# A fused attention and two-MLP kernel: seven products per tile pair in another order

## The chip, the cores and the metric

One Trainium2 chip, one core of it. The metric is the device time of one execution in microseconds (us). Before the change it is 658.96 us, the median of three runs (658.83 to 658.99).

## What is computed

All data are float32. The output of one layer is the input of the next:

```python
scores = q @ k.T / 8 - log(448);  attn = 1 / (1 + exp(-scores));  x = attn @ v    # 4 x 12 heads, 448 x 64
x = max(x @ w1, x @ w2, x @ w3) @ moe_w_out                                      # 1792 x 768, inner 768
h = x @ moe2_w_in                                                                 # 1792 x 1024
solu = h * softmax(h);  ln = (solu - mean) / sqrt(var + 1e-6) * g_ln
out = ln @ moe2_w_out                                                             # 1792 x 768
```

The change lies in the second MLP, in the product that gives `h`.

## The kernel before, in words

**Stages.** Attention runs first. In its course the kernel multiplies `moe_w_out` by `moe2_w_in`, so that the first MLP's maximum feeds `h` directly through a merged weight. Then come the three products of the first MLP with their maximum (`product`, line 634, and `sums`, line 652). The second layer has two stages: stage L gives `h` (with softmax and normalization behind it), stage O gives the output.

**Products.** Every large product is a seven-product scheme of the Strassen-Winograd kind on 2 x 2 blocks. A unit is a pair of token tiles (256 rows), and there are seven units, numbered 0 to 6 (called L0 to L6 in stage L, O0 to O6 in stage O). The seven products P1 to P7 of a unit each multiply one of seven token operands (A11, A12, S2, S1, S3, A22, S4) by one of seven weight operands; `PROD` (line 38) has the pairs. Every operand is split into a high and a low part, and a block takes three matmuls (high-high, high-low, low-high). A product is 9 matmuls of 512 columns in stage L and 12 of 384 columns in stage O (`product_c`, line 940).

**Running sums.** X collects P1, then P6, then P7, then P4. After P1, P6 and P7 ScalarE copies the sum as it stands (lines 1122, 1142, 1153), and after P4 it is read once more. The next product into X has to wait until the copy has read it. V collects P5, then P3, and is read by VectorE after P5 and after P3. Z holds P2. PSUM has three buffers for X, two for V, two for Z.

**Order of the work around the change.** The loop from line 1169 walks over groups: L0 to L6, then O0 with O1 together, then O2 to O6. A group of stage L runs on TensorE, with the last two products of the unit before in its first half: P1 of this unit (`begin`), P4 (`fourth`) and P3 (`third`) of the unit before (both called in `close`, line 1109), P2 (`second`), P6 (`sixth`), P5 (`fifth`), P7 (`seventh`). The orders of TensorE, ScalarE and VectorE are those of the program's text, and each of them takes its instructions in that order.

**Background work.** Two queues of small steps are woven between the matmuls. `bg` holds `prep` (line 788), which makes the seven operands of the next unit: ScalarE casts the high part (line 51), VectorE subtracts for the low part (line 56) and forms sums (line 59). `lazy` holds `solu_ln` (line 980): two Exp, two multiplies, two Square, some tiny steps, two Identity, two transposes, and the write of the result to DRAM, from which stage O's operands are loaded (`load_u`, line 1027). `third` of a unit of stage L puts that unit's `solu_ln` into `lazy` as its last act. After each matmul `pace` (line 934) adds 0.227 (L) or 0.174 (O) to a credit, and while it is positive one step is called and its cost taken off (0.56 or 0.69 for a step of `prep`, 1.32 for a multiply, 1.25 for a transpose, 0.78 for reading a finished sum by VectorE):

```python
while credit["t"] > 0:
    if not step(bg) and not step(lazy):
        credit["t"] = 0.0
```

So `lazy` gets a step only where `bg` has none that can be done, and credit is dropped where both are empty. `prep` of the next unit is put into `bg` after five products of a group (line 1206). If a product finds its operand not made yet, `product_c` calls steps of `bg` until it is (line 943). The operands lie in a ring of ten buffers (`place`, line 757). One of stage O takes two, so each takes over the buffers of the operand five places before it, and can be made only when the product that uses that one has been issued. `in_turn` (line 842) alternates between the `prep` of O0 and of O1.

Of the kernel before, what the change touches and what calls it, by code (L numbers as in the profile page):

```python
# [44 lines left out]
def sigmoid_attention_max_moe_solu_ln(tc, q, k, v, w123, wo, wi, w2, g, out):  # L45
# [12 lines left out]
    def tt(dst, a, b, op):  # L58
        dve.tensor_tensor(out=dst, in0=a, in1=b, op=op)
# [8 lines left out]
    def shut(*cms):  # L68
        for cm in cms:
            cm.__exit__(None, None, None)  # L70
# [563 lines left out]
    def product(ps, u, name, start, stop):  # L634
        gi, bp = u
        a, bn = PROD[name]
        while (gi, a) not in wops or any((bp, bn, c) in fts for c in range(3)):
            run_bg()
        wt = wops[(gi, a)]
        for c in range(3):  # L640
            xh, xl = xops[bp][(bn, c)]
            wh, wl = (wt[:, i, c * P : (c + 1) * P] for i in range(2))
            for i, (l, r) in enumerate(((wh, xh), (wh, xl), (wl, xh))):
                pe.matmul(ps, lhsT=l, rhs=r, start=(start and c == 0 and i == 0), stop=(stop and c == 2 and i == 2), skip_group_check=True)  # L644
                tick["n"] += 1
                if c == 2 and i == 2:
                    used[(gi, a)] = used.get((gi, a), 0) + 1
                while tick["done"] < tick["n"] * tick["rate"]:
                    run_bg()
                    tick["done"] += 1  # L650
# [73 lines left out]
    def weight_slots(name, tags, side="left"):  # L724
        cm, p = open_pool(name, 1, side=side)
        slot_pools.append(cm)
        return {tag: p for tag in tags}
# [9 lines left out]
    def load_wf(nm, tag):  # L737
        t = wfs[("L", nm)] = wslot[tag].tile([P, 3, 2, 512], F32R, tag=f"s{tag}", name=f"wf{nm}")
        pool.dma_start(out=t.bitcast(F32).rearrange("p c a b -> p c (a b)"), in_=w_d[nm][:, :, : 2 * 512])
# [181 lines left out]
    def step(queue):  # L921

        while queue:
            cost = next(queue[0], "end")
            if cost == "end":
                queue.popleft()
                continue
            if cost is None:
                return False
            credit["t"] -= cost  # L930
            return True
        return False
# [7 lines left out]
    def product_c(ps, kind, p, name, start, stop):  # L940
        a, bn = PROD[name]
        key = (kind, p, a)
        while key not in cops:
            assert step(bg), key
        hl = cops.pop(key)
        wt = wfs[(kind, bn)]
        chunks, dt = (3, 0.227) if kind == "L" else (4, 0.174)
        for c in range(chunks):
            for i, (l, m) in enumerate(((0, 0), (0, 1), (1, 0))):
                pe.matmul(  # L950
                    ps,
                    lhsT=hl[l][:, c * P : (c + 1) * P],
                    rhs=wt[:, c, m],
                    start=(start and c == 0 and i == 0),
                    stop=(stop and c == chunks - 1 and i == 2),
                    skip_group_check=True,
                )
                if c == chunks - 1 and i == 2:
                    spent.add(key)
                pace(dt)  # L960

    def charge(cost):
        credit["t"] -= cost
# [9 lines left out]
    def add_min(dst, ps, other, low, first):  # L973

        dve.tensor_tensor_reduce(
            out=dst, in0=ps, in1=other, scale=-1.0, scalar=first, op0=ALU.add, op1=ALU.min, accum_out=low
        )
        charge(0.78)
# [48 lines left out]
    def load_u(p):  # L1027
        for t in tiles[2 * p : 2 * p + 2]:
            while t not in turned:
                step(bg)  # L1030
                assert step(lazy), t
            ut = (hfirst if p == 0 else tp).tile([P, 4, 256], F32, tag="hu", name=f"ut{t}", bufs=2 if p == 0 else 11)
            sp.dma_start(out=ut, in_=u_d[t].rearrange("b f i e -> (b f) i e"))
            uts[t] = ut.rearrange("p i (k t) -> p k i t", k=K2)
# [23 lines left out]
    def put_out(p, i, j, t):  # L1058
        r = tiles[2 * p + i]
        sp.dma_start(out=out[r * P : (r + 1) * P, j * HU : (j + 1) * HU], in_=t)  # L1060
# [12 lines left out]
    def release(kind, p, name):  # L1073

        if (kind, p) == ("L", NP2 - 1):
            n = LOADS.index(PROD[name][1])
            if n + 1 < len(LOADS):
                load_w2(LOADS[n + 1], n)

    def fourth(o):  # L1080
        kind, p = o["kind"], o["p"]
        cx = o["at"][3]
        product_c(o["X"], kind, p, "P4", False, True)
        release(kind, p, "P4")
        if kind == "L":
            first, low = (x[:, 1:] for x in sts[p][:2])
            dve.tensor_scalar(
                out=cx, in0=o["X"], scalar1=-1.0, scalar2=first, op0=ALU.mult, op1=ALU.min, accum_out=low
            )
            charge(0.78)  # L1090
        else:
            act.copy(cx, o["X"])
            put_out(p, 1, 0, cx)

    def third(o):
        kind, p = o["kind"], o["p"]
        u2 = o["at"][1]
        product_c(o["V"], kind, p, "P3", False, True)
        release(kind, p, "P3")
        if kind == "L":  # L1100
            first, low = (x[:, :1] for x in sts[p][:2])
            add_min(u2, o["V"], u2, low, first)
            lazy.append(solu_ln(p))
        else:
            tt(u2, o["V"], u2, ALU.add)
            charge(0.56)
            put_out(p, 0, 1, u2)

    def close(units):

        if len(units) == 1:
            fourth(units[0])
        for o in units:
            third(o)

    def begin(kind, p):
        w = 512 if kind == "L" else HU
        at = targets(kind, p)
        X = ps_x.tile([P, 512], F32, tag="x", name=f"X{kind}{p}")[:, :w]
        product_c(X, kind, p, "P1", True, False)  # L1120
        release(kind, p, "P1")
        act.copy(at[0], X)
        return dict(kind=kind, p=p, X=X, at=at, w=w)
# [15 lines left out]
    def sixth(o):  # L1139
        product_c(o["X"], o["kind"], o["p"], "P6", False, False)  # L1140
        release(o["kind"], o["p"], "P6")
        act.copy(o["at"][1], o["X"])
# [25 lines left out]
    prev = None  # L1168
    for n, (kind, g) in enumerate(groups):
        p, last = g[-1], n == len(groups) - 1  # L1170
        if prev and len(prev) > 1:
            for o in prev:
                fourth(o)
        now_open = [begin(kind, g[0])]
        if n == 0:
            product(old["X"], old["u"], "P4", False, True)
            sums(old["u"], 1, 0, old["X"], None)
            product(old["V"], old["u"], "P3", False, True)
            sums(old["u"], 0, 1, old["V"], old["u2"])
            for cm in (xat_cm, xau_cm, xa_cm, st_cm, raw_cm):  # L1180
                shut(cm)
            wslot.update(weight_slots("sc", (5, 6, 7), side="right"))
            for tag in (5, 6):
                load_wf(LOADS[tag], tag)
            t_cm, tp = open_pool("tp", 2, side="right")
            act.preload_act_table_set("natural_log_exp_and_others")
        else:
            close(prev)
        now_open += [begin(kind, p) for p in g[1:]]
        if n == 2:  # L1190
            load_w2(LOADS[0], 7)
        if (kind, p) == ("L", NP2 - 1):
            load_u(1)
        if not last:
            for o in now_open:
                second(o)
        if (kind, p) == ("O", 1):
            load_u(2)
        for o in now_open:
            sixth(o)  # L1200
        if kind == "L":
            if p + 2 < NP2:
                next_h(p + 2)
            if p == NP2 - 2:
                load_u(0)
            bg.append(prep_l(p + 1) if p + 1 < NP2 else in_turn(prep_o(0), prep_o(1), 1))
        elif not last:
            bg.append(prep_o(p + 1))
            if 1 < p < NP2 - 2:
                load_u(p + 2)  # L1210
        for o in now_open:
            fifth(o)
        for o in now_open:
            seventh(o)
        if (kind, p) == ("O", 1):
            load_u(3)
        if last:
            for o in now_open:
                second(o)
        prev = now_open  # L1220
# [61 lines left out]
```

## Time and profile before

| what | value |
|---|---|
| device time, median of 3 runs | 658.96 us |
| the profiled execution's own time | 658.38 us |
| its span, first to last instruction | 656.6 us |
| TensorE matmul busy | 637.8 us, 97% |
| VectorE busy | 490.7 us, 75% |
| ScalarE busy | 373.4 us, 57% |
| stage L, first product to the first of stage O | 427 to 544 us |
| stage O, to the end | 544 to 656.6 us |
| mean granted TensorE clock | 0.992 |

Busy shares are means over the whole span; in a timeline a row's number in front is its start in us from the span's start, then its duration, and in brackets the time the engine was idle before it and what released it.

### The profile page before, as it was taken

Reading aid. Unit: us, or ns where it says so; the run is one execution under the profiler, and the core shown is the slowest. Engines: PE = TensorE matmul, PEld = TensorE weight load, DVE = VectorE, ACT = ScalarE, POOL = GpSimd, SP = SyncE. Lnnn points to the kernel's source line nnn. Section 1 sums busy time; section 2 is a strip of 40 time slices with the busy share of each in tenths; the row PEclk is TensorE's granted clock in tenths of the full one; section 3 lists DMA queues with packets and bytes.
Section 4 is the critical chain, followed back from the end, with each engine's and each line's share of the span. In section 5 each row is a group of like instructions: output and inputs, shape, how many; then the busy total and the mean of one; then the engine's idle time right before and its main releaser. Section 6 shows DMA issues by size and latency. Waiting matters only on the chain.

```text
span 656.6 us, 9719 instructions
## 1 busy us (share of the span) xinstructions
PE 637.8 (97%) x3283; PEld 519.3 (79%) x3283; DVE 490.7 (75%) x1070; ACT 373.4 (57%) x712; POOL 72.6 (11%) x147
## 2 busy tenths in 40 slices
PE   9999999999999999999999999977999999999897
PEld 6555588754557999999999999955877889999897
DVE  4799987599547788886888678544688879687672
ACT  5888523578866545455455454222666674766551
POOL 2111121000100101101101100112000035300000
PEclk9999999999999999999999999997999999999999
DMA  8688668853710346765468543899336269956151
GB/s 292 216 256 260 220 199 303 314 211 109 259 33 0 105 125 188 215 166 163 131 176 233 168 121 90 248 374 407 130 108 182 58 205 385 311 180 185 59 168 70
DMA packets 85921, 125.17 MB, mean 191 GB/s; under 512 B 39024, under 2 KB 65648, under 8 KB 85872
## 3 DMA queue, kind: packets, MB, share of 16 engines
q1 hardware_dynamic: 74288, 70.84, 34.2%
q0 software_dynamic: 11440, 53.48, 25.2%
q8 instruction: 26, 0.43, 0.3%
q10 hardware_dynamic: 144, 0.23, 0.1%
q14 instruction: 23, 0.19, 0.1%
HBM read 84.15 MB, written 40.37 MB: 190 GB/s over the span
## 4 chain that ended last, share of the span: by engine, by line
PE 65%; DVE 16%; ACT 6%; DMA 6%; issue 5%; SPq 1%; POOL 0%; DVEq 0%; ACTq 0%; POOLq 0%
PE x L644 19%; PE v L644 9%; PE XO L950 7%; PE av L272 6%; PE z L644 5%; PE XL L950 5%; PE sc L251 4%; PE VO L950 4%; PE VL L950 2%; PE ZO L950 2%; DMA wfT<-w_dT 2%; ACT e L998 2%; PE sc L247 1%; DMA wfB<-w_dB 1%; ACT h L1014 1%
## 5 line engine op out<-in xcount | busy, mean ns | idle before, releaser
L272 PE MATMUL av<-sf,vr 128*64 128x448 f32 x384 | 77.5, 545 | 0.0
L259 ACT ACTIVATE sf<-sc,bias_s 128x896 f32<-128x896 f32 x72 | 67.9, 1013 | 2.4
L141 POOL DMA_DIRECT2D raw<-in_w x52 | 28.0, 539 | 277.3 <-DVE S L56 138.4
L272 PEld LDWEIGHTS av<-sf,vr 128*64 128x64 f32 x384 | 25.4, 136 | 40.9 <-issue 34.4
L251 PE MATMUL sc<-qt,kt 64*128 64x448 f32 x432 | 51.1, 375 | 1.5 <-ACT sf L256 1.5
L473 PE MATMUL pw<-wi_t,r_wo 128*128 128x512 f32 x216 | 49.6, 390 | 0.0
L251 PEld LDWEIGHTS sc<-qt,kt 64*128 64x128 f32 x432 | 39.0, 184 | 11.7 <-issue 4.3
L473 PEld LDWEIGHTS pw<-wi_t,r_wo 128*128 128x128 f32 x216 | 40.4, 188 | 9.4 <-issue 1.0
L689 ACT COPY u<-x 128x448 f32<-128x448 f32 x36 | 19.1, 530 | 44.3 <-PE x L644 44.3
L950 PE MATMUL XL<-wfT,c_L_S 128*128 128x512 f32 x126 | 33.1, 409 | 4.1 <-DMA wfT<-w_dT 3.1
L644 PE MATMUL x<-T3h,S 128*128 128x448 f32 x108 | 33.7, 366 | 0.0
L644 PE MATMUL x<-B11h,A 128*128 128x448 f32 x108 | 33.7, 366 | 0.0
L644 PE MATMUL x<-T4h,A 128*128 128x448 f32 x108 | 33.6, 365 | 0.0
L644 PE MATMUL x<-T2h,S 128*128 128x448 f32 x108 | 33.6, 365 | 0.0
L644 PE MATMUL v<-B22h,S 128*128 128x448 f32 x108 | 33.6, 365 | 0.0
L644 PE MATMUL z<-B21h,A 128*128 128x448 f32 x108 | 33.6, 365 | 0.0
L644 PE MATMUL v<-T1h,S 128*128 128x448 f32 x108 | 33.6, 365 | 0.0
L950 PEld LDWEIGHTS XL<-wfT,c_L_S 128*128 128x128 f32 x126 | 24.3, 196 | 11.3 <-issue 4.2
L413 ACT ACTIVATE raw<-raw,g_sb 128x192 f32<-128x192 f32 x32 | 13.3, 466 | 31.3 <-DVE raw L157 31.3
L950 PE MATMUL XO<-w2tT,c_O_S 128*128 128x384 f32 x168 | 31.1, 336 | 0.0
L157 DVE SCALAR_TENSOR_TENSOR raw<-raw 128x384 int32<-128x384 int32 x52 | 29.0, 557 | 1.1
L950 PEld LDWEIGHTS XO<-w2tT,c_O_S 128*128 128x128 f32 x168 | 29.3, 188 | 0.0
(185 smaller groups left out, 1547.1 us busy)
## 6 DMA issues: line engine op xcount, KB each, us to landing
raw<-in_w POOLq DMA_DIRECT2D x52, 384.0 KB, 4.1
w_d<-w2s SPq DMA_DIRECT2D x48, 192.0 KB, 2.4
u_d<-h SPq DMA_DIRECT2D x56, 128.0 KB, 2.9
ut<-u_d SPq DMA_DIRECT2D x14, 512.0 KB, 5.3
kr<-in_k SPq DMA_DIRECT2D x24, 256.0 KB, 3.5
vr<-in_v SPq DMA_DIRECT2D x24, 256.0 KB, 3.9
raw<-in_wi POOLq DMA_DIRECT2D x16, 384.0 KB, 4.9
w_dT<-wsT SPq DMA_DIRECT2D x12, 512.0 KB, 3.7
```

Source lines behind the costliest of these rows:

```text
L141: pool.dma_start(out=t, in_=source(key).rearrange("p (n t) -> p n t", t=2))
L157: dve.scalar_tensor_tensor(out=yi, in0=raws[key][:, cols, 0], scalar=29, in1=yi, op0=ALU.logical_shift_right, op1=ALU.bitwise_or)
L247: pe.matmul(sc[:, 0, :S], lhsT=kt[:, x, c * P :], rhs=qt[:, y], start=start, stop=stop)
L251: pe.matmul(sc[:, j, :S], lhsT=kt[rows, x, c * P : (c + 1) * P], rhs=qt[rows, y], start=start, stop=stop)
L259: act.activation(sf, sc[:, :, :S], AF.Sigmoid, bias=bias_s, scale=1.0 / math.sqrt(D))
L272: pe.matmul(pa[j * D : (j + 1) * D, :S], lhsT=vr[:, j, c], rhs=sf if c == 3 else sf[:, j], start=(n == 0), stop=(n == 3),)
L413: act.activation(half, half, AF.Copy, scale=g_sb[:, kc + 4 * i : kc + 4 * i + 1])
L473: pe.matmul(ps, lhsT=wt[:, a, cols], rhs=wi_t[:, b, c0 : c0 + 512], start=(i == 0), stop=(i == 3 * KC - 1))
L644: pe.matmul(ps, lhsT=l, rhs=r, start=(start and c == 0 and i == 0), stop=(stop and c == 2 and i == 2), skip_group_check=True)
L689: act.copy(e, ps)
L950: pe.matmul(ps, lhsT=hl[l][:, c * P : (c + 1) * P], rhs=wt[:, c, m], start=(start and c == 0 and i == 0), stop=(stop and c == chunks - 1 a ...
L998: act.activation(e[i], h[i], AF.Square, bias=su[:, c], scale=-float(F2), accum_out=vs[:, c])
```

## The change

In stage L, from the second unit on, P4 and P3 of the unit before no longer follow P1 directly. P4 goes behind P2, P3 behind P6. The order P1, P4', P3', P2, P6, P5, P7 (a prime marks the unit before) becomes P1, P2, P4', P6, P3', P5, P7. The group in which O0 begins still closes L6 as before, and stage O's order is not touched. `prep` of the next unit still goes into `bg` after five products; the step that puts `solu_ln` of the unit before into `lazy` now stands directly ahead of that, where it had stood two products ahead. No instruction is added or removed.

```diff
             t_cm, tp = open_pool("tp", 2, side="right")
             act.preload_act_table_set("natural_log_exp_and_others")
-        else:
+        elif kind == "O":
             close(prev)
         now_open += [begin(kind, p) for p in g[1:]]
...
         if (kind, p) == ("O", 1):
             load_u(2)
+        if n > 0 and kind == "L":
+            fourth(prev[0])
         for o in now_open:
             sixth(o)
+        if n > 0 and kind == "L":
+            third(prev[0])
         if kind == "L":
```

## Rows read from the trace of the kernel before

**Rows 1.** The page, part 1: busy time, share of the span, instructions.

```profile
PE   637.8 (97%) x3283; PEld 519.3 (79%) x3283; DVE 490.7 (75%) x1070; ACT 373.4 (57%) x712; POOL 72.6 (11%) x147
```

**Rows 2.** Waits of PE from 440 us on: total, times, longest.

```profile
PE VL L950 <- DMA wfB<-w_dB: 1.9, 1, 1.9
PE XO L950 <- ACT u L1153: 1.7, 1, 1.7
PE XL L950 <- ACT h L1153: 0.4, 1, 0.4
```

**Rows 3.** Timeline of PE, 435 to 463 us: P2, P6, P5, P7 of L0, and on.

```profile
435.01 2.35 PE L950 MATMUL ZL<-wfB,c_L_A 128*128 128x512 f32 x9 [1.92 <-DMA wfB<-w_dB]
...
440.12 3.09 PE L950 MATMUL XL<-wfT,c_L_S 128*128 128x512 f32 x9 [2.77 <-DMA wfT<-w_dT]
445.57 4.21 PE L950 MATMUL VL<-wfT,c_L_S 128*128 128x512 f32 x9 [2.35 <-DMA wfT<-w_dT]
450.07 3.04 PE L950 MATMUL XL<-wfT,c_L_S 128*128 128x512 f32 x9 [0.29 <-DMA wfT<-w_dT]
452.95 2.22 PE L950 MATMUL XL<-wfB,c_L_A 128*128 128x512 f32 x9
455.02 2.29 PE L950 MATMUL XL<-wfT,c_L_A 128*128 128x512 f32 x9
459.21 2.32 PE L950 MATMUL VL<-wfB,c_L_S 128*128 128x512 f32 x9 [1.89 <-DMA wfB<-w_dB]
461.36 2.22 PE L950 MATMUL ZL<-wfB,c_L_A 128*128 128x512 f32 x9
```

**Rows 4.** Timeline of PE: P5 and P7 of L2, P1 of L3.

```profile
479.93 2.23 PE L950 MATMUL VL<-wfT,c_L_S 128*128 128x512 f32 x9
483.12 2.33 PE L950 MATMUL XL<-wfT,c_L_S 128*128 128x512 f32 x9 [0.96 <-ACT h L1142]
485.29 2.23 PE L950 MATMUL XL<-wfB,c_L_A 128*128 128x512 f32 x9
```

**Rows 5.** Timeline of ACT just before that: the second Exp and the copy behind it.

```profile
481.37 1.14 ACT L988 ACTIVATE e<-h,st 128x1024 f32<-128x1024 f32 x1
482.50 0.56 ACT L1142 COPY h<-XL 128x512 f32<-128x512 f32 x1
```

**Rows 6.** Timeline of ACT: the first Exp of L0, and L6's first square and its Identity.

```profile
462.36 1.15 ACT L988 ACTIVATE e<-h,st 128x1024 f32<-128x1024 f32 x1 [6.56 <-DVE st L975]
...
614.38 1.15 ACT L998 ACTIVATE e<-h,st 128x1024 f32<-128x1024 f32 x1
...
618.63 2.37 ACT L1014 ACTIVATE h<-h,st 128x1024 f32<-128x1024 f32 x2 [1.02 <-DVE st L1010]
```

**Rows 7.** Timeline, 572 to 574 us: O2's first two casts, and its P1.

```profile
572.16 1.14 ACT L51 CAST c_O_A<-ut 128x512 fp32r<-128x512 f32 x2
573.67 2.27 PE L950 MATMUL XO<-w2tB,c_O_A 128*128 128x384 f32 x12
```

**Rows 8.** Groups by line: busy us, mean ns of one, idle before and its releaser.

```profile
L1018 DVE STREAM_TRANSPOSE h<-h 128x1024 f32<-128x1024 f32 x14 | 17.3, 1240 | 7.3 <-ACT h L1014 7.3
L56 DVE TENSOR_TENSOR c_O_A<-ut,c_O_A 128x512 fp32r<-128x512 f32 x21 | 14.3, 686 | 5.8 <-ACT c_O_A L51 4.5 <-PE VO L950 1.0 <-PE ZO L950 0.2
L51 ACT CAST c_O_A<-ut 128x512 fp32r<-128x512 f32 x21 | 12.7, 618 | 0.9 <-PE VO L950 0.9
L59 DVE TENSOR_TENSOR u<-VO,u 128x384 f32<-128x384 f32 x14 | 7.7, 550 | 10.1 <-ACT u L1153 5.9 <-PE VO L950 4.0
```

**Rows 9.** Timeline of PE and ACT: two products of stage O, and the copy of the first.

```profile
611.21 2.24 PE L950 MATMUL XO<-w2tT,c_O_S 128*128 128x384 f32 x12
613.29 2.24 PE L950 MATMUL VO<-w2tT,c_O_S 128*128 128x384 f32 x12
613.49 0.48 ACT L1142 COPY u<-XO 128x384 f32<-128x384 f32 x1 [3.54 <-PE XO L950]
```

**Rows 10.** A window of 1 us: PE, PEld, DVE, ACT, POOL busy, then granted clock.

```profile
442.00:443.00 1.00, 1.00 (x3) 0.40 (x2) 0.00 (x0) 0.00 (x0) 0.00 (x0) 0.50 1.07 423
```

## The prediction

> **What bounds the kernel now.** I read the page's busy shares first [rows 1]: TensorE is busy for 97% of the span, so a reordering can at most return the gaps, and any new gap is paid in full. Then the waits of TensorE, which say what the gaps are [rows 2]. From 440 us on, the change can reach one wait of 1.9 us for a weight's transfer and the waits for a ScalarE copy of a running sum: 0.4 us and one of 1.0 us in stage L [rows 4], 1.7 us in stage O. Then the timeline at two of them. At 459.21 us P3 of L0 waits for its weight [rows 3]. At 483.12 us P7 of L2 waits for the copy behind P6 [rows 4], and the copy is late only because an Exp of `solu_ln` stands ahead of it in ScalarE's queue [rows 5]. So it is background work, not the copy's own 0.56 us, that holds TensorE, and where that work is issued decides what the change is worth.
>
> **What is taken away.** A product of stage L starts 2.07 us after the one before it (452.95 to 455.02) [rows 3].
> 1. P3 of L0 moves behind P1, P2 and P6 of L1 and P4 of L0. In the old order it could have started at 457.1 us; in the new one its turn comes two products later, at 461.2 us, after the weight's arrival at 459.2 us. From 455.02 to 461.36 us are 6.34 us for two products that need 4.14: 2.2 us gone [rows 3]. The weight's load is issued by POOL, whose order is not touched, and SP's loads of the next rows still go out after five products, so I cost both moves at nothing; their cover is a whole group of some 14 us.
> 2. P7 of L2: 485.29 less 479.93 is 5.36 us for two products, 1.2 us over [rows 4]. The wait for the copy behind P7, 0.4 us by the view, is some 0.7 us by the same count (start-up is 0.25 us there). Two more on copies, too short for the view, are at most 0.5 us each; I take 0.8 together. With one more product between, all are covered: 2.7 us.
>
> In sum 4.9 us are to be had; the lower bound is 2.2, if ScalarE falls further behind.
>
> **What is moved with it: the background account.** P3's last act puts the unit's `solu_ln` into the lazy queue. In the old order two products (18 x 0.227 = 4.1 of credit) followed before the next unit's `prep` went in ahead of it. In the new order `prep` follows at once. So in the group of L1 both queues run empty while P4, P6 and P3 go by, and the credit is dropped; the loss is never made up, since a group gives 63 x 0.227 = 14.3 and asks for four readings (3.1), a `prep` (6.3) and a `solu_ln` (6.7), 16.1 in all. I carried the account step by step through both orders with the program's own costs. For the old order it puts the first Exp of L0 into P2 of L1, which ends at 463.4 us, and the squares of L6 behind P6 of O4 as steps forced by the load of their tiles; the trace has them there [rows 6]. For the new order it gives, at the end of L6, the `solu_ln` of L3 not yet finished, where before that of L4 had begun: some 2.7 of cost later. What is late next are stage O's operands, at five places.
>
> The prices: a cast 0.62, a subtraction or sum 0.69, a transpose 1.24, a VectorE reading 0.55 us [rows 8]; a product of stage O takes 2.08 us, its copy 0.48, and the copy starts 0.2 us after the product's end (613.49 against 613.29) [rows 9]. A product's first two matmuls (0.35 us) need the high part alone.
> 1. P1 of O0: between P6 of L6 and the cast of A11 ScalarE now has a copy, the whole tail of L3's `solu_ln` from the first square to the second Identity, and the cast. The tail of L6 takes 6.6 us (614.38 to 621.00), of which VectorE's small steps are 1.0 [rows 6]. So 0.2 + 0.5 + 6.6 + 0.6 = 7.9 us, against P3, P5, P7 = 6.2 us on TensorE. With the low part (0.69 - 0.35) a wait of 2.1 us; 2.3 with start-up.
> 2. P1 of O2: its buffers are those of the operand five places before. In the old order that is A22 of O0, so the cast ran at 572.16 us, 1.5 us ahead of P1 [rows 7]. In the new order the two alternating preparations come out otherwise, and it is A22 of O1, free only at the end of P4 of O1, directly ahead of P1. ScalarE is then still at two Identity and a copy. From the end of P7 of O0 it has four copies (1.9), the tail without VectorE's part (5.6) [rows 6] and two casts (1.1) [rows 7]: 8.6 us, some 8.4 as neighbours overlap a little, against three products, 6.2 us. Behind the second Identity, transpose and subtraction on VectorE end 0.5 us after copy, cast and the first two matmuls (1.24 + 0.69 - 0.48 - 0.62 - 0.35): 2.7 us.
> 3. P2 of O2: A12 needs P3 of O1 issued, then reading 0.55, sum 0.69, subtraction 0.69, with 0.2 ahead and 0.35 off: 1.8; 2.0 with start-up.
> 4. P6 of O2: reading, two sums, cast, subtraction after P2's end: 0.2 + 0.55 + 1.4 + 0.6 + 0.35 = 3.1 us.
> 5. P1 of O3: copy, reading, subtraction: 0.2 + 0.48 + 0.55 + 0.69 - 0.35 = 1.6 us.
>
> With 0.6 us for three small ones: 12.3 us. The old 1.7 us wait stays: the squares of L6 are forced at the same place. Bounds: a quarter less (9.2), if chains overlap better than end to end, and a fifth more (14.8), if ScalarE's queue is longer than I count.
>
> **The clock.** Nowhere in stage O does the trace before show gaps so close, so I bound this from both sides. In L0 the granted clock went from 1.00 to 0.50 (2.4 to 1.2 GHz) after waits of 1.9 and 2.8 us with one product between [rows 3, 10], and was back at 452.95 us, where a product takes 2.22 us again. P6, P5 and P7 took 3.09, 4.21 and 3.04 us instead of 2.22 each: 3.7 us [rows 3]. The waits of 1.0 and 1.7 us [rows 2, 4], and the single one of 1.89 us at 459.21 us, where the product behind took 2.32 us [rows 3], cost no clock. Places 3 and 4 are 2.0 and 3.1 us with one product between, which is nearest to L0; but three products then run without a break, where L0 had two more waits in them. I take half, 1.7 us, between 0 and 3.7.
>
> The Trainium skill, TensorE: Matmul & The Clock Gate, A second HAM failure mode: psum-queue depth-cycling, has frequent short idles between groups of matmuls swing the clock between its levels; by it the sum would carry not one fall but several, up to the last rival below. The trace agrees only in part: the single waits just named left the clock alone.
>
> **The sum.** -4.9 + 12.3 + 1.7 = 9.1 us. The profiled execution's own 658.38 us becomes 667.5 (its span 665.7). It lies 0.6 us below the median, so 668.1 us, called 668.0.
>
> **The rivals.**
> - *The clock holds.* Operands are late as above and nothing else: 658.96 + 7.4 = 666.4 us. For it: 6.2 us of unbroken work before place 3. Against: L0.
> - *The clock falls and stays.* Rising only after the wait at place 5, it costs L0's full 3.7 us: 670.1 us. For it: the waits at 3, 4 and 5 come 8 us apart at most, as in L0.
> - *The other side: the operands stay hidden.* If operands of O2 are cast before their products as in the old order [rows 7], the gaps go and none comes: 658.96 - 4.9 = 654.1 us. It decides at P1 of O2: a cast of its A11 ahead of the end of P4 of O1 would show it. For it: VectorE is only 75% busy [rows 1]. Against: steps are placed by credit and ring, not by who is idle.
> - *It does nothing.* The copies stay late because Exp and squares move along with them, and only the 2.2 us at 459 us are gained and lost again at O0: 659 us. Against: the account's four places in O2 and O3.
> - *The clock swings all along*, low from place 2 to place 5: eight products of 2.08 us take twice that, 7.4 + 16.6, 683 us. For it: four waits in 24 us. Against: between places 2 and 3 lie three products without a break. It is the case that the Trainium skill's section above would give.
>
> **How the numbers follow.** Forecast 0.42, clock holds 0.30, clock falls and stays 0.13, clock swings 0.03, hidden 0.07, nothing 0.05 (0.02 same, 0.03 slower). Low end: no clock term, waits a quarter shorter, 658.96 - 4.9 + 9.2 = 663.3, taken to 662.5 for a start-up counted double. High end: 658.96 - 4.9 + 14.8 + 3.7 = 672.6. Outside lie the last three rivals and a little beside: under 0.2. 0.2%, 1.3 us, is about what a measurement of this kernel can tell from no change: faster 0.07, same 0.02, slower 0.91.
>
> **What would show it.** Right: P3 of L0 without a wait; no wait on line 1142 or 1153 in stage L; new waits of P1 of O0 and of P1, P2, P6 of O2 and P1 of O3 on casts or subtractions (lines 51, 56); the first Exp of L0 in P2 of L2. The forecast is wrong if these five are absent or under 6 us together, if stage L loses time, or if the clock drops elsewhere.

## The result, and the profile after

The changed kernel takes 668.11 us (median of 4 runs, 667.82 to 668.71); the kernel before, beside it, 658.98 us. The ratio is 1.013, 95% interval 1.0112 to 1.0149: slower by 9.1 us. The profiled execution has 667.82 us of its own and a span of 666.0 us, 9.4 more than before. The matmuls are the same ones; the page's first part, which answers to [rows 1]:

```profile
PE   639.1 (96%) x3283; PEld 518.1 (78%) x3283; DVE 490.3 (74%) x1070; ACT 373.4 (56%) x712; POOL 72.5 (11%) x147
```

TensorE's busy time grew by 1.3 us only, so some 8 of the 9.4 are idle time. The waits of TensorE from 420 us on (total, times, longest), less those of the first unit of stage L, answer to [rows 2]:

```profile
PE XO L950 <- ACT c_O_A L51: 4.3, 3, 1.7
PE XO L950 <- ACT c_O_S L51: 2.6, 1, 2.6
...
PE XO L950 <- ACT u L1153: 1.7, 1, 1.7
...
PE ZO L950 <- DVE c_O_A L56: 1.5, 1, 1.5
PE XO L950 <- DVE c_O_A L56: 0.6, 2, 0.4
PE XO L950 <- DVE c_O_S L56: 0.3, 1, 0.3
```

The waits on copies in stage L (1.0 and 0.4 us [rows 4, 2]) and the 1.9 us for the weight of P3 of L0 are gone. In their place stand waits for casts (line 51) and subtractions (line 56), all of buffers with `O` in the name: operands of stage O. The timeline of TensorE shows where:

```profile
454.23 2.41 PE L950 MATMUL XL<-wfB,c_L_A 128*128 128x512 f32 x9
...
462.67 2.25 PE L950 MATMUL VL<-wfB,c_L_S 128*128 128x512 f32 x9
...
539.18 2.23 PE L950 MATMUL XL<-wfT,c_L_S 128*128 128x512 f32 x9
542.90 0.62 PE L950 MATMUL XO<-w2tB,c_O_A 128*128 128x384 f32 x2 [1.49 <-ACT c_O_A L51]
543.79 2.00 PE L950 MATMUL XO<-w2tB,c_O_A 128*128 128x384 f32 x10 [0.27 <-DVE c_O_A L56]
545.63 2.24 PE L950 MATMUL XL<-wfT,c_L_A 128*128 128x512 f32 x9
...
564.33 0.52 PE L950 MATMUL XO<-w2tT,c_O_S 128*128 128x384 f32 x2
565.16 4.08 PE L950 MATMUL XO<-w2tT,c_O_S 128*128 128x384 f32 x22 [0.31 <-DVE c_O_S L56]
569.08 4.50 PE L950 MATMUL XO<-w2tT,c_O_A 128*128 128x384 f32 x24
575.27 0.62 PE L950 MATMUL XO<-w2tB,c_O_A 128*128 128x384 f32 x2 [1.70 <-ACT c_O_A L51]
576.24 2.02 PE L950 MATMUL XO<-w2tB,c_O_A 128*128 128x384 f32 x10 [0.35 <-DVE c_O_A L56]
578.11 4.32 PE L950 MATMUL VO<-w2tB,c_O_S 128*128 128x384 f32 x24
582.47 0.61 PE L950 MATMUL ZO<-w2tB,c_O_A 128*128 128x384 f32 x2
584.61 2.01 PE L950 MATMUL ZO<-w2tB,c_O_A 128*128 128x384 f32 x10 [1.53 <-DVE c_O_A L56]
589.24 2.73 PE L950 MATMUL XO<-w2tT,c_O_S 128*128 128x384 f32 x12 [2.62 <-ACT c_O_S L51]
591.81 2.24 PE L950 MATMUL VO<-w2tT,c_O_S 128*128 128x384 f32 x12
593.89 2.25 PE L950 MATMUL XO<-w2tT,c_O_S 128*128 128x384 f32 x12
597.22 2.75 PE L950 MATMUL XO<-w2tB,c_O_A 128*128 128x384 f32 x12 [1.09 <-ACT c_O_A L51]
599.81 2.24 PE L950 MATMUL XO<-w2tT,c_O_A 128*128 128x384 f32 x12
...
630.87 2.35 PE L950 MATMUL XO<-w2tT,c_O_A 128*128 128x384 f32 x12 [1.70 <-ACT u L1153]
```

A product split in two rows (x2 and x10) is one that began on the high part and then waited for the low part. Read it from start to start, taking off 2.07 us for each product of stage L and 2.08 for each of stage O, so that start-up is counted with the wait:

| stretch | over pace | forecast |
|---|---|---|
| P1 of L1 to the end of P7 of L6: 454.23 to 541.25, 42 products | 0.1; before 4.3 | gain of 4.9 |
| P1 of O0: 541.25 to 545.63 | 2.3 | 2.3 |
| P7 of O0 and of O1: 564.33 to 569.08 | 0.6 | 0.6 for three small ones, place not named |
| P4 of O0 and of O1, P1 of O2: 569.08 to 578.11 | 2.8 | 2.7 |
| P2 and P6 of O2 with what lies ahead: 578.11 to 591.81 | 5.4 | 2.0 + 3.1 |
| P7 of O2, P1 of O3: 593.89 to 599.81 | 1.8 | 1.6 |

The new gaps are 12.8 us (forecast 12.3), and stage L gives back 4.2. The other 1.3 us lie ahead of all this: P1 of L1 starts at 454.23 us, where it started at 452.95 [rows 3]. In that stretch nothing was changed. With the 0.4 us by which stage O was over pace before, 1.3 - 4.2 + 12.8 - 0.4 = 9.5 against the measured 9.4.

Why the operands are late is seen on ScalarE's timeline, which answers to [rows 6, 7]:

```profile
472.45 1.15 ACT L988 ACTIVATE e<-h,st 128x1024 f32<-128x1024 f32 x1
...
539.96 2.37 ACT L1014 ACTIVATE h<-h,st 128x1024 f32<-128x1024 f32 x2 [1.02 <-DVE st L1010]
542.24 1.65 ACT L51 CAST c_O_A<-ut 128x512 fp32r<-128x512 f32 x3
...
571.96 2.38 ACT L1014 ACTIVATE h<-h,st 128x1024 f32<-128x1024 f32 x2
574.23 0.47 ACT L1092 COPY cx<-XO 128x384 f32<-128x384 f32 x1
574.59 0.63 ACT L51 CAST c_O_A<-ut 128x512 fp32r<-128x512 f32 x1
...
623.84 1.15 ACT L998 ACTIVATE e<-h,st 128x1024 f32<-128x1024 f32 x1
```

The first Exp of L0's `solu_ln` runs at 472.45 us, in P2 of L2, a group later than before (462.36). At 542.24 the casts for P1 of O0 come straight behind two Identity left over from stage L (the fourth unit's pair, so L3's), which end at 542.3, when TensorE has been idle for some 1 us. At 574.59 the cast for P1 of O2 stands behind two more Identity and a copy; before, it ran 1.5 us ahead of its product [rows 7], and now ends with TensorE waiting. At 623.84 us the squares of L6 still come behind P6 of O4, and the old 1.7 us wait follows at 630.87.

### The profile page after: what moved, and what is told of

It reads as the page before. It is cut to its first block, busy times and chain, and to the rows that moved or that the text cites. A ratio compares the mean times of both kernels' runs of the same rounds, so it can differ in the third digit from the quotient of the medians.

```text
span 666.0 us, 9722 instructions
## 1 busy us (share of the span) xinstructions
PE 639.1 (96%) x3283; PEld 518.1 (78%) x3283; DVE 490.3 (74%) x1070; ACT 373.4 (56%) x712; POOL 72.5 (11%) x147
## 4 chain that ended last, share of the span: by engine, by line
PE 69%; DVE 15%; issue 6%; ACT 5%; DMA 4%; POOL 0%; SPq 0%; ACTq 0%; DVEq 0%; POOLq 0%
PE x L644 18%; PE v L644 9%; PE XL L950 8%; PE XO L950 7%; PE av L272 5%; PE z L644 5%; PE sc L251 4%; PE VL L950 3%; PE VO L950 3%; PE ZO L950 2%; PE ZL L950 2%; DMA wfT<-w_dT 1%; PE sc L247 1%; ACT e L998 1%; DVE y_wi L157 1%
## 5 line engine op out<-in xcount | busy, mean ns | idle before, releaser
L251 PEld LDWEIGHTS sc<-qt,kt 64*128 64x128 f32 x432 | 38.4, 184 | 12.3 <-issue 4.6
```

The costliest lines, as they stand in the source:

```text
L251: pe.matmul(sc[:, j, :S], lhsT=kt[rows, x, c * P : (c + 1) * P], rhs=qt[rows, y], start=start, stop=stop)
```

## The experiments

Two theories were set against each other. **Theory A, the background account:** what costs time is that `solu_ln` of L0 reaches the lazy queue directly ahead of `prep`, so that the group of L1 finds both queues empty, drops its credit, and background work stays behind until stage O's operands are late. **Theory B, the order of the products:** the new order by itself is slower, through the later P4 and P3, whatever the background does. The first four ran beside runs of the kernel before of 659.33 us (658.31 to 661.27), the last four beside 659.81 us (658.38 to 663.43). Ratios are to those.

### The old order, with only the queueing of solu_ln moved (e1)

Edit to the kernel before:

```diff
+    late = []
...
-            lazy.append(solu_ln(p))
+            (lazy if p == NP2 - 1 else late).append(solu_ln(p))
...
         if kind == "L":
+            lazy.extend(late)
+            late.clear()
```

> The kernel before with its own order of products; only the moment at which a unit's softmax work enters the lazy queue is moved to where the changed kernel has it (two products later). Theory A (the loss comes from the background work falling behind): slower than before by 3 to 6 us, 662 to 665 us, with a new wait at P1 of O2 on a cast, the wait on the copy behind P6 of L6 grown to some 2 us, and the copy waits of O3 and O4 grown; less than the changed kernel's 9 us, since the readings of finished sums take their credit at other places and the two orders do not come out alike. Theory B (the new order of products itself costs the time, by holding X and V of the unit before longer): the same as before, 659 us.

Measured: 666.65 us (665.25 to 667.81), ratio 1.011 (1.0093 to 1.0126). With no product moved, nearly as much is lost as by the change. The size was missed by some 2 us, and the timeline of TensorE says why:

```profile
456.60 2.33 PE L951 MATMUL XL<-wfT,c_L_A 128*128 128x512 f32 x9 [0.98 <-ACT h L1123]
460.89 3.88 PE L951 MATMUL VL<-wfB,c_L_S 128*128 128x512 f32 x9 [1.96 <-DMA wfB<-w_dB]
...
627.75 3.67 PE L951 MATMUL XO<-w2tT,c_O_A 128*128 128x384 f32 x12 [3.76 <-ACT u L1154]
```

and in windows of 1 us (columns as in [rows 10]; the two behind the granted clock are the DMA engines' share and GB/s):

```profile
462.00:463.00 1.00, 1.00 (x4) 0.77 (x3) 0.00 (x0) 0.00 (x0) 0.19 (x1) 0.50 1.04 399
...
629.00:630.00 1.00, 1.00 (x5) 1.00 (x4) 1.00 (x4) 0.00 (x0) 0.00 (x0) 0.50 0.95 225
```

P3 of L0 waits 1.96 us, as before, but here the product ahead of it waited too; it takes 3.88 us where it took 2.32 [rows 3]. P4 of O4 takes 3.67 where the changed kernel has 2.35. These are products at the lower clock, granted 0.50, some 3 us together. Of the five places only P1 of O2 has a wait, the one foreseen on a cast, and it is small (0.42 us). The others are three on copies in stage L (0.98, 0.56 and 1.24 us, the last foreseen at some 2), one on an operand at P6 of O5 (0.74), and the wait of P4 of O4, grown from 1.7 to 3.76 us. So moving the background work back is enough to lose this much, but where it is lost depends on the order of the products too. This run supports A and does not by itself show that A is the whole of the change.

### The new order from L2 on only (e2)

Edit to the changed kernel:

```diff
-        elif kind == "O":
+        elif kind == "O" or n == 1:
             close(prev)
...
-        if n > 0 and kind == "L":
+        if n > 1 and kind == "L":
             fourth(prev[0])
...
-        if n > 0 and kind == "L":
+        if n > 1 and kind == "L":
             third(prev[0])
```

> The changed kernel, but the group of L1 closes L0 in the old order; the new order begins with L2. Theory A, with the account's detail that the loss is the credit dropped in the group of L1 alone: the waits of O0, O2 and O3 go (one of under 1 us may stay at P1 of O2), the copy waits of stage L stay away, the 2 us wait of P3 of L0 for its weight is back: 2.7 us less 0.9, so 656 to 658 us, faster than before. Theory A without that detail (each group loses): 665 us or more. Theory B: 667 us, five of the six regrouped units still being in the new order.

Measured: 657.17 us (656.20 to 658.27), ratio 0.9968 (0.9956 to 0.9980). The waits of TensorE from 454 us on are two in all:

```profile
PE XO L950 <- ACT u L1153: 1.7, 1, 1.7
PE VL L950 <- DMA wfB<-w_dB: 1.5, 1, 1.5
```

Five of six groups have the new order, and neither a copy nor an operand of stage O holds TensorE. For these five, Theory B falls: the whole loss hangs on the group of L1. Whether it is the order there or the credit, the next two tell.

### The new order, credit not dropped in the group of L1 (e3), and kept up to 2.0 (e6)

Edits to the changed kernel; the line marked e6 stands in e6 alone:

```diff
-    credit = {"t": 0.0}
+    credit = {"t": 0.0, "keep": False}
...
             if not step(bg) and not step(lazy):
+                if credit["keep"]:
+                    credit["t"] = min(credit["t"], 2.0)     # e6
+                    return
                 credit["t"] = 0.0
...
+        credit["keep"] = n == 1
```

> The changed kernel, but credit is not dropped in the group of L1 when both queues are empty, so the steps missed there are called later in the same group. Theory A: the background work catches up in one burst, with one wait of 1 to 2 us for it in L2; the waits of O0, O2 and O3 go but for one under 1 us: 4.9 us less 2 to 3, so 656 to 658 us. Theory B: unchanged against the changed kernel, 668 us.

> The changed kernel with the credit kept in the group of L1, but at most 2.0 of it. Theory A: as with all of it kept, but the burst is smaller, so the wait of 1.6 us that a copy had behind it in L2 goes, and one of about 1 us for the operand of P1 of L4 comes: 655.5 to 657 us, some 1 us under the kernel that keeps all. Theory B: 668 us.

Measured: e3 657.22 us (655.98 to 661.87, 12 runs), ratio 0.9972 (0.9956 to 0.9988); e6 655.80 us (654.45 to 657.13, 6 runs), ratio 0.9935 (0.9911 to 0.9959). The order of the products is that of the changed kernel in both. The waits of TensorE from 454 us on, of e3:

```profile
PE XO L952 <- ACT u L1155: 1.7, 1, 1.7
PE XL L952 <- ACT h L1124: 1.6, 1, 1.6
```

and of e6:

```profile
PE XO L953 <- ACT u L1156: 1.7, 1, 1.7
```

Only the dropped credit differs, and a loss of 9 us turns into a gain: this is the experiment that names the cause, and with it Theory B falls for the group of L1 too. In e3 the kept credit may be spent all at once when `solu_ln` arrives, and a copy in L2 comes late (1.57 us at P6 of L2, 476.37 us). With the credit held to 2.0 that wait goes as well. The one foreseen at P1 of L4 is there, too short for the view: the product ahead of it and P1 itself take 4.85 us, 0.7 over pace. e6 is faster than both kernels, by 4.0 us against the one before.

How much credit is lost can be counted by stepping through the program with its own costs (no trace shows credit). From the group of L1 to the end of stage L it is 2.4 in the kernel before, 3.4 in e3, where all of it goes in L2, 3.7 to 3.9 in e2, e5, e6 and e7, 5.0 in e1, and 5.8 in the changed kernel and e4. So some credit is dropped in every one of them; the three kernels that lost time are those with 5.0 and more.

### The preparations of O0 and O1 alternate from the second on (e4)

Edit to the changed kernel:

```diff
-            bg.append(prep_l(p + 1) if p + 1 < NP2 else in_turn(prep_o(0), prep_o(1), 1))
+            bg.append(prep_l(p + 1) if p + 1 < NP2 else in_turn(prep_o(0), prep_o(1), 2))
```

> The changed kernel, but the alternation between the preparation of O0 and O1 starts one step later, which changes who takes which buffers of the ring; the background work is as late as in the changed kernel. Theory A with the ring's part (O2's operands wait because five places before them lies A22 of O1): the waits at P1, P2 and P6 of O2 and at P1 of O3 nearly go, the one at P1 of O0 stays at 2.3 us, and the late work shows up as a longer copy wait at P4 of O4, some 4 to 5 us instead of 1.7: 662 to 665 us. Theory A without the ring's part: the four waits stay, 668 us. Theory B: 668 us.

Measured: 664.06 us (661.81 to 664.33), ratio 1.0064 (1.0048 to 1.0079). P1 of O0 waits as in the changed kernel (1.50 us), but the waits of O2 and O3 are gone. So those four hang on how the two preparations alternate. Stepped through, the program puts A11 of O2 over A22 of O0 before, over A22 of O1 in the changed kernel, as the prediction had it, and over S3 of O1 in e4; the edit moves the order of the steps along with the ring, so the two are not told apart. But the work that had been late there is late elsewhere, on the timeline of TensorE:

```profile
621.24 4.21 PE L950 MATMUL XO<-w2tT,c_O_A 128*128 128x384 f32 x12 [4.26 <-ACT u L1153]
625.24 2.87 PE L950 MATMUL VO<-w2tB,c_O_S 128*128 128x384 f32 x12
```

and in windows of 1 us just ahead of that product:

```profile
619.00:620.00 1.00, 0.00 (x0) 0.00 (x0) 0.28 (x1) 1.00 (x2) 0.00 (x0) 0.86 0.00 0
620.00:621.00 1.00, 0.00 (x0) 0.00 (x0) 1.00 (x2) 1.00 (x2) 0.00 (x0) 0.50 0.00 0
```

P4 of O4 waits 4.26 us instead of 1.7, the granted clock falls to 0.50 while TensorE is idle, and two products take 2.6 us more than on pace; P6 of O5 waits 0.74 us. Mending one place of a queue that is behind moves the loss; e3 and e6, which mend the account, remove it.

### P3 ahead of P6: in the group of L1 (e5), and in every group (e7)

e5 queues `solu_ln` of L0 one product earlier, e7 does so for every unit. Edits to the changed kernel, e5 and then e7:

```diff
+        if n == 1:
+            third(prev[0])
         for o in now_open:
             sixth(o)
-        if n > 0 and kind == "L":
+        if n > 1 and kind == "L":
             third(prev[0])
```

```diff
-        for o in now_open:
-            sixth(o)
         if n > 0 and kind == "L":
             third(prev[0])
+        for o in now_open:
+            sixth(o)
```

> The changed kernel, but in the group of L1 alone P3 of L0 stands ahead of P6 of L1 instead of behind it. Theory A: the softmax work of L0 is queued one product earlier, so less credit is dropped, the account comes out as in the old order from O0 on but for one wait under 1 us at P1 of O2; P3 of L0 still comes after its weight's arrival, give or take 0.5 us; one wait of about 1 us for the operand of P1 of L4. 4.9 us less 2 to 2.5: 656 to 657 us, faster than before. Theory B (the order of products): 667 to 668 us, as the changed kernel.

> The changed kernel with P3 of the unit before ahead of P6 in every group, so that P6 and P7 have one product between them again, as in the old order. Theory A: the background work is not late in stage O, but a copy behind P6 that stands behind a tail of softmax work holds P7 again: one wait of 2 to 3 us on the copy behind P6 in L3 and one of 0.5 us in L6, where the changed kernel has none in stage L: 656 to 658.5 us. If the second product between P6 and P7 is not what took those waits away, stage L has none here either: 654 to 655 us. Theory B: 664 to 668 us.

Measured: e5 657.04 us (655.99 to 659.46, 12 runs), ratio 0.9960 (0.9945 to 0.9975); e7 659.48 us (657.60 to 660.67, 10 runs), ratio 0.9987 (0.9968 to 1.0005). One product between the queueing and `prep` is enough to remove the loss: in e5 the first Exp of L0 runs at 463.72 us, in the group of L1 again. e7 came out about 1 us above what was expected. Its largest wait, foreseen at 2 to 3 us, and one that was not foreseen, on the timeline of TensorE:

```profile
460.96 2.32 PE L950 MATMUL VL<-wfB,c_L_S 128*128 128x512 f32 x9 [1.05 <-DMA wfB<-w_dB]
...
498.64 2.34 PE L950 MATMUL XL<-wfT,c_L_S 128*128 128x512 f32 x9 [2.32 <-ACT h L1142]
```

and on that of ScalarE:

```profile
495.75 2.37 ACT L1014 ACTIVATE h<-h,st 128x1024 f32<-128x1024 f32 x2 [1.09 <-DVE st L1010]
498.03 0.56 ACT L1142 COPY h<-XL 128x512 f32<-128x512 f32 x1
```

The copy behind P6 stands behind two Identity that themselves waited for VectorE. The other is P3 of L0, which comes one product earlier than in the changed kernel and waits 1.05 us for its weight. That is about the size of the miss; the profile is of one execution, so it is not shown that it is the whole of it.

### The changed kernel once more (e8)

No edit.

> The changed kernel once more, beside the others on one chip. Theory A: 667 to 669 us, and the same five places of waits in stage O to 0.1 us each, while the start of P1 of L1 differs from the first profile by up to 1 us, since the clock and the weights' transfers in L0 vary from run to run. If the 1.3 us by which P1 of L1 started later in the changed kernel's profile belong to the change, it starts at 454.2 us again.

Measured: 669.61 us (666.19 to 671.23, 4 runs), ratio 1.0137 (1.0101 to 1.0172). The waits at the five places are those of the first profile to within 0.03 us. What differs is the clock. The timeline of TensorE:

```profile
573.14 0.62 PE L950 MATMUL XO<-w2tB,c_O_A 128*128 128x384 f32 x2 [1.69 <-ACT c_O_A L51]
574.11 3.28 PE L950 MATMUL XO<-w2tB,c_O_A 128*128 128x384 f32 x10 [0.36 <-DVE c_O_A L56]
...
588.38 3.84 PE L950 MATMUL XO<-w2tT,c_O_S 128*128 128x384 f32 x12 [2.63 <-ACT c_O_S L51]
```

and windows of 1 us in it:

```profile
575.00:576.00 1.00, 1.00 (x5) 1.00 (x4) 1.00 (x3) 0.36 (x2) 0.00 (x0) 0.50 0.94 250
...
578.00:579.00 1.00, 1.00 (x8) 1.00 (x7) 0.00 (x0) 1.00 (x3) 0.00 (x0) 1.00 0.30 97
...
589.00:590.00 1.00, 1.00 (x5) 0.89 (x4) 0.65 (x2) 0.00 (x0) 0.00 (x0) 0.50 0.94 356
```

The ten matmuls of P1 of O2 take 3.28 us where the first profile has 2.02, and P6 takes 3.84 where it has 2.73: 2.4 us. The first profile has the full clock at the same place, within its P6 of O2:

```profile
590.00:591.00 1.00, 1.00 (x6) 1.00 (x7) 0.52 (x1) 0.00 (x0) 0.00 (x0) 1.00 1.01 385
```

P1 of L1 starts at 452.24 us in this profile, at 454.23 in the first, and between 452.12 and 454.41 in all ten profiles, although the order of the work up to there is the same in all of them. So the 1.3 us of the first profile are a difference between executions and no effect of the change. For e8 the same sum, with the first profile's gaps, reads -0.7 (start) - 4.2 + 12.8 - 0.4 + 2.4 = 9.9 us, against the 9.7 by which its span of 666.3 us is longer.

## Why the prediction was right

The forecast was 668.0 us, and 668.1 was measured, in the forecast direction and through the forecast mechanism. That the two agree to 0.1 us is luck: the forecast has 1.7 us of clock where the first profile has none, and the first profile has 1.3 us of a later start that the forecast does not have. By its steps:

1. **P3 of L0 and the copies (4.9 us taken away): right, a little too large.** No product from P1 of L1 to P7 of L6 waits any more. There were 4.3 us over pace to be had, and 4.2 came. The 0.8 for the short waits on copies was the term set too high.
2. **The background account: right, and shown.** The loss hangs on the credit dropped in the group of L1: giving L1 its old order (e2), its credit (e3, e6), or one product of distance (e5) each removes the loss. The trace has L0's first Exp in P2 of L2 and the squares of L6 where they were, as forecast.
3. **The five places: right.** All five are there, with 12.8 us against 12.3. P6 of O2 is the largest miss, 0.3 us with P2. Of the three small ones only one is found, and it takes the 0.6 us of all three. e4 shows that the four in O2 and O3 hang on the alternation, of which the ring is a part; the one at P1 of O0 stays there, as its working by ScalarE's queue would have it.
4. **The clock (1.7 us): half of a range from 0 to 3.7, a value that no profile shows.** It is 0 in the first profile and 2.4 in e8, where the first fall comes at P1 of O2, ahead of the places 3 and 4 at which the forecast looked for it. So the mechanism of the rival "the clock holds" is what the first profiled execution did, and its time came out near the forecast because P1 of L1 started 1.3 us later there. What the forecast lacked is that the cost of these waits changes from one execution to the next; its range covered that.

   The Trainium skill, TensorE: Matmul & The Clock Gate, A second HAM failure mode: psum-queue depth-cycling, was cited for a clock that swings with short idles: the trace of e8 agrees, with two falls to 0.50 and two recoveries to 1.00 between 573 and 593 us, and the first profile, with the same waits and 1.00 throughout, does not.

Of the rivals, "it does nothing" and "the clock swings all along" are off by 9 and 15 us; the 3.7 us of "the clock falls and stays" were not reached in either profile, e8 having 2.4. They are not excluded for other executions: two of e8's four took 671.16 and 671.23 us, some 3 us more than the one profiled, and have no trace. "The operands stay hidden" put a gain of 4.9 us on the case in which no operand of stage O comes late. That is the case that e6 makes, and it gains 4.0.

What stays open: why the clock fell at P1 and P6 of O2 in one execution and not in another with the same waits, and what sets the start of P1 of L1.

## What to carry to other kernels

Where background steps are woven in by a credit, moving a product also moves the moment at which the next work becomes available; ask for each moved call what it queues, whether both queues can run empty in between, and what becomes of the credit then. A loss of credit early shows up much later, at the first place where the steps have a hard deadline, here 80 us on; so carry the account through to the end before trusting a reordering that removes every wait in its own stage. And mend the account, not the place: with up to 2.0 of credit kept, the same reordering that lost 9 us gains 4.

## What was not expected of the hardware

- The same 1.9 to 2.0 us wait of P3 of L0 left the clock alone before (the product took 2.32 us [rows 3]) and was followed by a product of 3.88 us in e1, where the product ahead had waited 0.98 us.
- Single waits of 3.76 and 4.26 us at P4 of O4 (e1, e4) were followed by products of 3.67 and 4.21 us; the wait of 1.7 us at that place never was, in any profile.
- Equal waits, equal to 0.03 us, gave 0 and 2.4 us of clock loss in two executions of one kernel, and the start of stage L's second unit moved by 2.3 us between profiles with the same code ahead of it.
